# A last matrix product with the two halves of its moving operand side by side, and the sums of a block at other slots

## The chip, the core and the metric

The kernel runs on one core of a Trainium2 chip. The metric is the device time of one execution in microseconds. Three runs of the kernel before took 1485.69, 1486.63 and 1486.93 us; the median is 1486.63 us.

## What is computed

A retention layer (attention with a decay in place of a softmax), then two feed-forward layers over 4608 tokens. The change touches only the last product, `g @ w_out` of the second one.

```
x = attention output, (4608, 512)                     # 8 batches of 576 positions, 8 heads of 64
h = (x @ w1) * (x @ w2) @ w3;  x2 = h @ w_out         # 512 -> 1024 -> 512
h = x2 @ w_in                                         # 512 -> 2048
g = h * clip(h + 3, 0, 6) / 6
out = g @ w_out2                                      # 2048 -> 512
```

All inputs are normal random numbers times a scale.

## The kernel before

Precision. TensorE multiplies in a format with a shorter mantissa than float32 (float32r). Each operand is therefore split into a high and a low part, `hi` (ScalarE casts the value) and `lo` (VectorE subtracts `hi` from the value), and a product is the sum of three matmuls: hi x hi, hi x lo and lo x hi. The helper `mm3` (lines 123 to 127) issues these three, each with its own load of the stationary operand.

The last product. The 2x2 block products of `g @ w_out2` are formed with seven products in place of eight (a Strassen form). `out_block(b)` (lines 886 to 930) makes 256 tokens, and there are 18 blocks. In a block, product p (0 to 6) has an operand made from four pieces of g (128 tokens by 1024 features each, called `raw`, one load each) and their sums as the stationary side, and a prepared matrix T of w_out2 as the moving side, 1024 x 256 as `hi` and `lo`. Line 920 cuts from T, for each of the eight steps kt of 128 features, 512 columns: 256 of `hi` and 256 of `lo` beside them. Line 921 gives the two halves to `mm3` as two moving operands of 256 columns. A step is thus three loads and three matmuls of 256 columns; a block has 7 x 8 = 56 steps and the stage 18 x 56 = 1008.

Banks. Four PSUM banks A, B, C and D take the seven products: A products 0 and 3, B product 1, D products 2 and 5, C products 4 and 6. Where a bank is used twice, the second product adds to what is there, after the first result has been read. Before, 256 of the 512 columns of a bank are used. The pool has eight banks, so a block and the next one use different ones. After each product its bank is read: by ScalarE (a copy) for products 0 and 3 (lines 923 and 925), by VectorE (an add of the bank to an earlier result, line 695) for the other five. The results are `u`, `U = u + B`, `V = U + D` and four pieces of the output; after products 5 and 6 SP's queue stores 128 tokens each (line 900).

Operands. `prep(b, p, s)` (lines 835 to 854) makes `hi` (line 845, ScalarE) and `lo` (line 849, VectorE, through line 130) of product p, 128 x 1024 values each; it is called two products ahead. There are three pairs of operand tiles, so the tile of product p + 2 is that of product p - 1. `s_sum(b, i)` (lines 825 to 831) is one of four sums of a block, 128 x 1024 values on VectorE: sums 1 and 2 go to the units 1 and 2 for products 2 and 1, sum 3 to unit 1 for product 4, sum 4 to unit 1 for product 5. `load_raw` (line 813) loads a piece of the next block on SP's queue.

Order. The kernel is scheduled by hand. Every step begins with a tick; `at(s, f)` (line 113) says that f is issued at tick s, ahead of the matmuls of that step, and engines run their instructions in the order of issue. The read of a product stands at the tick after its last step; `hi` one tick and `lo` three ticks after the start of the product in which they are prepared; sums 3 and 4 at the start of products 2 and 3 (line 852), sums 1 and 2 of the next block five ticks into products 4 and 5 (line 916); the loads of the next block at the start of product 0 (three pieces) and four ticks into product 3 (one).

Of the kernel before, what the change touches and what calls it, by code (L numbers as in the profile page):

```python
# [7 lines left out]
F32 = mybir.dt.float32  # L8
# [18 lines left out]
def retention_moe_kernel(  # L27
# [20 lines left out]
    nc = tc.nc  # L48
# [61 lines left out]
    now = [0]  # L110
    ready = set()

    def at(s, f):
        slots.setdefault(max(s, now[0]), []).append(f)

    def tick():
        q_ = slots.get(now[0], [])
        while q_:
            q_.pop(0)()
        slots.pop(now[0], None)  # L120
        now[0] += 1

    def mm3(out_ap, sh, sl, mh, ml, first, last, **kw):
        tick()
        nc.tensor.matmul(out=out_ap, lhsT=sh, rhs=mh, start=first, stop=False, **kw)  # L125
        nc.tensor.matmul(out=out_ap, lhsT=sh, rhs=ml, start=False, stop=False, **kw)  # L126
        nc.tensor.matmul(out=out_ap, lhsT=sl, rhs=mh, start=False, stop=last, **kw)  # L127

    def sub(eng, out_ap, x, y):
        eng.tensor_tensor(out=out_ap, in0=x, in1=y, op=ALU.subtract)  # L130
# [45 lines left out]
    A, Bh = slice(0, 64), slice(64, 128)  # L176
# [125 lines left out]
    with tc.manual_schedule():  # L302
# [155 lines left out]
        for n, (i, j) in enumerate(w3_order()):  # L458
            if j == 0:
                Wps[i] = ps_mm.tile([128, DM], F32, tag="mm", name="Wps")  # L460
            ps = Wps[i]
# [3 lines left out]
                             start=j == 0, stop=j == KF - 1)  # L465
# [219 lines left out]
        ps = ctx.enter_context(tc.tile_pool(name="ps", bufs=8, space=PSUM))  # L685
# [8 lines left out]
        def add(out_ap, a, b):  # L694
            nc.vector.tensor_tensor(out=out_ap, in0=a, in1=b, op=ALU.add)  # L695
# [106 lines left out]
        def f32_unit(k):  # L802
            if k not in un:
                un[k] = ring(k, [128, 1024], F32, "unit")
            return un[k]

        def raw(b, h, kh):
            return f32_unit(RAW[(4 * b + PARTS.index((h, kh))) % 7])

        def load_raw(b, h, kh):  # L810
            if b < NB3:
                p0 = 256 * b + 128 * h
                nc.sync.dma_start(out=raw(b, h, kh).rearrange("p (m t) -> p m t", t=128), in_=gd[:, 8 * kh:8 * kh + 8, p0:p0 + 128])

        def op_tiles(q):
            i = q % 3
            if i not in ops:
                if i == 0:
                    ops[i] = [wf_p.tile([128, 1024], F32R, tag="wr", name="op") for _ in range(2)]
                else:  # L820
                    x = xo_p.tile([128, 2, 1024], F32R, tag=("xh", "xl")[i - 1], name="op")
                    ops[i] = [x[:, 0], x[:, 1]]
            return ops[i]

        def s_sum(b, i):
            if b < NB3:
                o, x, y, f = (
                    (1, (1, 0), (1, 1), ALU.add), (2, 1, (0, 0), ALU.subtract),
                    (1, (0, 0), (1, 0), ALU.subtract), (1, (0, 1), 2, ALU.subtract))[i - 1]
                t = [f32_unit(v) if isinstance(v, int) else raw(b, *v) for v in (x, y)]  # L830
                nc.vector.tensor_tensor(out=f32_unit(o), in0=t[0], in1=t[1], op=f)  # L831
# [3 lines left out]
        def prep(b, p, s):  # L835
            b, p = b + p // 7, p % 7
            if b == NB3:
                return
            c = {}

            def src():
                return f32_unit(SRC[p]) if isinstance(SRC[p], int) else raw(b, *SRC[p])

            def hi():
                nc.scalar.copy(out=op_tiles(7 * b + p)[0], in_=src())  # L845

            def lo():
                h, l = op_tiles(7 * b + p)
                sub(nc.vector, l, src(), h)

            if p in (4, 5):
                at(s, lambda: s_sum(b, p - 1))
            at(s + 1, hi)
            at(s + 3, lo)

        for sb in range(NSB):
            for k, n in enumerate(SETS):
                if (sb, k) == (NSB - 1, 7):
                    s = now[0]
                    at(s + 5, lambda: s_sum(0, 2))  # L860
                    prep(0, 1, s + 9)
                    at(s + 9, lambda: load_raw(0, 0, 1))
                run_set(sb, n)
                if sb < NSB - 1:
                    k0 = 3 if sb == 0 else 2
                    if k0 <= k < k0 + 4:
                        load_xop(sb + 1, k - k0)
                    if k == 7:
                        for i in range(4, 7):
                            at(now[0], lambda i=i, sb=sb: load_xop(sb + 1, i))  # L870
                else:
                    if 1 <= k <= 4:
                        q_tile(k - 1)
                    if k == 2:
                        for part in PARTS[:3]:
                            load_raw(0, *part)
                    if k == 4:
                        s_sum(0, 1)
                    if k == 5:
                        prep(0, 0, now[0])  # L880
                    if k > 4:
                        q_late(k - 5)
# [3 lines left out]
        def out_block(b):  # L886
            c = {}
            z = b % 2
            o = [stg[:, 1024 * z + 512 * h:1024 * z + 512 * h + 512] for h in range(2)]
            u, U, V = (stg_hi[:, 512 * i + 256 * z:512 * i + 256 * z + 256] for i in range(3))  # L890
            p0 = 256 * b

            def bank(k):
                c[k] = ps.tile([128, 512], F32, tag="b", name="po")[:, 0:256]

            def store(h):
                hh, g = divmod((p0 + 128 * h) % (2 * BLK), BLK)
                g += (p0 + 128 * h) // (2 * BLK) * BLK
                r0 = g // HB1 * BLK1 + hh * HB1 + g % HB1
                nc.sync.dma_start(out=out[r0:r0 + 128, :], in_=o[h])  # L900

            def add2(out_ap, a, k):
                return lambda: add(out_ap, a, c[k])

            for p, (k, first) in enumerate((
                    ("A", True), ("B", True), ("D", True), ("A", False), ("C", True), ("D", False), ("C", False))):
                if first:
                    bank(k)
                if p == 0:
                    for part in PARTS[:3]:  # L910
                        at(now[0], lambda part=part: load_raw(b + 1, *part))
                if p == 3:
                    at(now[0] + 4, lambda: load_raw(b + 1, 0, 1))
                prep(b, p + 2, now[0])
                if p in (4, 5):
                    at(now[0] + 5, lambda p=p: s_sum(b + 1, p - 3))
                h, l = op_tiles(7 * b + p)
                for kt in range(8):
                    ts = slice(128 * kt, 128 * kt + 128)
                    w = tq[p, kt // 2][:, 512 * (kt % 2):512 * (kt % 2) + 512]  # L920
                    mm3(c[k], h[:, ts], l[:, ts], w[:, 0:256], w[:, 256:512], first and kt == 0, kt == 7, skip_group_check=True)
                if p == 0:
                    at(now[0], lambda: nc.scalar.copy(out=u, in_=c["A"]))
                elif p == 3:
                    at(now[0], lambda: nc.scalar.copy(out=o[0][:, 256:512], in_=c["A"]))
                else:
                    at(now[0], add2(*{1: (U, u, "B"), 2: (V, U, "D"), 4: (o[1][:, 0:256], V, "C"),
                                      5: (o[0][:, 0:256], U, "D"), 6: (o[1][:, 256:512], U, "C")}[p]))
                if p > 4:
                    at(now[0] + 1, lambda p=p: store(p - 5))  # L930

        for b in range(NB3):
            out_block(b)
# [66 lines left out]
```

## Time and profile before

| | |
|---|---|
| runs | 1485.69, 1486.63, 1486.93 us |
| the profiled execution's own time | 1486.61 us |
| its span, first to last instruction | 1484.7 us |
| mean granted TensorE clock | 0.999 of full speed |
| TensorE matmul / weight load busy | 1469.7 / 1313.3 us |
| VectorE / ScalarE / GpSimd busy | 956.4 / 568.8 / 254.2 us |
| matmuls of the last product | first at 1118.19 us, last at 1480.95 us |

PE stands for TensorE's matmuls, PEld for its weight loads, DVE for VectorE, ACT for ScalarE, POOL for GpSimd, SP for SyncE. A letter q behind a name is that engine's queue of DMA issues. Matmuls are pipelined: the duration of one is longer than the distance to the next, so that distances have to be read from the starts. L695 is line 695 of the kernel; a line can be that of a helper, and then the names of the tiles tell the use: `po` is a bank of the last product, `op` an operand tile, `unit` a piece of g or a sum, `wq` the matrix T, `stg` and `stghi` hold results. The kernel and the numbers of its lines are those of before.

### The profile page before, as it was taken

The numbers are of one execution on the slowest core, as the hardware profiler recorded it, in microseconds if no ns is written. First come the engines' busy times: TensorE is split into PE (matmuls) and PEld (weight loads), VectorE is DVE, ScalarE is ACT, GpSimd is POOL, SyncE is SP. The second block draws the span as 40 slices with busy tenths as digits, with TensorE's granted clock in tenths as the row PEclk, the third lists the DMA queues.
The fourth block names the chain that finished last, engine by engine and source line by source line (L and its number), as shares of the span: only waits on it lengthen the run. The fifth ranks groups of instructions, "written<-read, shape, count | busy, mean of one in ns | idle before, by whom it ended". The sixth has DMA issues, their size and how long they took to land. (4 is left out here: it accounts for less than half of the span.)

```text
span 1484.7 us, 26113 instructions
## 1 busy us (share of the span) xinstructions
PE 1469.7 (99%) x10544; PEld 1313.3 (88%) x10544; DVE 956.4 (64%) x1617; ACT 568.8 (38%) x857; POOL 254.2 (17%) x461
## 2 busy tenths in 40 slices
PE   9999999999999999999999999999999999999999
PEld 5478888888888888888889999999999999999998
DVE  6886566566564746574545666666667777777775
ACT  6563333233333333332433333333334333333332
POOL 3313212222222111110012322232220000000000
PEclk9999999999999999999999999999999999999999
DMA  9963657565565556554799753644698444455441
GB/s 327 264 179 107 204 166 190 180 178 191 170 191 155 198 163 194 168 163 140 261 354 348 280 221 149 256 175 189 241 389 253 131 127 120 122 142 143 138 131 45
DMA packets 186586, 287.34 MB, mean 194 GB/s; under 512 B 12528, under 2 KB 143600, under 8 KB 184928
## 3 DMA queue, kind: packets, MB, share of 16 engines
q1 hardware_dynamic: 103584, 151.01, 31.1%
q0 software_dynamic: 25856, 75.93, 16.6%
q10 hardware_dynamic: 57024, 58.73, 11.9%
q8 instruction: 83, 1.36, 0.4%
q14 instruction: 39, 0.32, 0.1%
HBM read 176.04 MB, written 109.58 MB: 192 GB/s over the span
## 5 line engine op out<-in xcount | busy, mean ns | idle before, releaser
L125 PE MATMUL po<-wq,op 128*128 128x256 f32 x1008 | 285.3, 283 | 0.0
L126 PE MATMUL po<-wq,op 128*128 128x256 f32 x1008 | 285.3, 283 | 0.0
L127 PE MATMUL po<-wq,op 128*128 128x256 f32 x1008 | 285.3, 283 | 0.0
L125 PE MATMUL pb<-xop,wset 128*128 128x384 f32 x672 | 226.2, 337 | 5.6 <-DVE stghi L695 2.4
L127 PE MATMUL pb<-xop,wset 128*128 128x384 f32 x672 | 225.8, 336 | 0.0
L126 PE MATMUL pb<-xop,wset 128*128 128x384 f32 x672 | 225.6, 336 | 0.0
L130 DVE TENSOR_TENSOR op<-unit,op 128x1024 fp32r<-128x1024 f32 x126 | 154.1, 1224 | 92.8 <-ACT op L845 92.8
L845 ACT CAST op<-unit 128x1024 fp32r<-128x1024 f32 x126 | 132.2, 1049 | 186.1 <-DVE unit L831 164.6
L127 PEld LDWEIGHTS po<-wq,op 128*128 128x128 f32 x1008 | 193.5, 192 | 0.0
L126 PEld LDWEIGHTS po<-wq,op 128*128 128x128 f32 x1008 | 193.5, 192 | 0.0
L125 PEld LDWEIGHTS po<-wq,op 128*128 128x128 f32 x1008 | 193.5, 192 | 0.0
L714 POOL DMA_DIRECT2D gd<-g x192 | 103.9, 541 | 348.7 <-DVE g L709 223.4
L186 POOL DMA_DIRECT2D qk<-in_qk_dram x144 | 84.3, 592 | 434.2 <-PE z L233 360.8
L705 ACT ACTIVATE stghi<-g,half 128x384 f32<-128x384 f32 x141 | 87.1, 617 | 132.7 <-DVE g L695 132.7
L125 PEld LDWEIGHTS pb<-xop,wset 128*128 128x128 f32 x672 | 126.2, 188 | 8.3 <-DVE stghi L695 3.0
L126 PEld LDWEIGHTS pb<-xop,wset 128*128 128x128 f32 x672 | 126.2, 188 | 0.0
L127 PEld LDWEIGHTS pb<-xop,wset 128*128 128x128 f32 x672 | 126.2, 188 | 0.0
L125 PE MATMUL pa<-xh,w1h 128*128 128x512 f32 x288 | 114.1, 396 | 0.0
L125 PE MATMUL px<-abh,Wh 128*128 128x512 f32 x288 | 114.0, 396 | 0.0
L126 PE MATMUL pa<-xl,w1h 128*128 128x512 f32 x288 | 112.2, 390 | 0.6 <-DVE xl L130 0.6
L125 PE MATMUL pb<-xh,w2h 128*128 128x512 f32 x288 | 112.3, 390 | 0.0
L127 PE MATMUL pa<-xh,w1l 128*128 128x512 f32 x288 | 112.2, 390 | 0.0
(137 smaller groups left out, 2542.1 us busy)
## 6 DMA issues: line engine op xcount, KB each, us to landing
gd<-g POOLq DMA_DIRECT2D x192, 192.0 KB, 4.0
unit<-gd SPq DMA_DIRECT2D x72, 512.0 KB, 5.7
xop<-xod SPq DMA_DIRECT2D x42, 768.0 KB, 9.0
qk<-in_qk_dram POOLq DMA_DIRECT2D x144, 128.0 KB, 4.6
wset<-wid SPq DMA_DIRECT2D x8, 1792.0 KB, 12.7
wr<-in_w_dram SPq DMA_DIRECT2D x24, 512.0 KB, 12.9
kv<-in_kv_dram POOLq DMA_DIRECT2D x36, 256.0 KB, 5.1
kv<-in_kv_dram POOLq DMA_DIRECT2D x72, 128.0 KB, 4.9
```

Source lines behind the costliest of these rows:

```text
L125: nc.tensor.matmul(out=out_ap, lhsT=sh, rhs=mh, start=first, stop=False, **kw)
L126: nc.tensor.matmul(out=out_ap, lhsT=sh, rhs=ml, start=False, stop=False, **kw)
L127: nc.tensor.matmul(out=out_ap, lhsT=sl, rhs=mh, start=False, stop=last, **kw)
L130: eng.tensor_tensor(out=out_ap, in0=x, in1=y, op=ALU.subtract)
L186: nc.gpsimd.dma_start(out=x[rows, g].rearrange("d x a i -> d x (a i)"), in_=qk[2 * t + g].rearrange("d x (b a) i -> d x b (a i)", a=2)[:, ...
L705: nc.scalar.activation(out=c["r"], in_=src(), func=ACTF.Relu, bias=half, scale=1.0 / 6.0)
L714: nc.gpsimd.dma_start(out=gd[:, m, p0:p0 + BLK], in_=c["g"])
L845: nc.scalar.copy(out=op_tiles(7 * b + p)[0], in_=src())
```

## The change

- A step of the last product is two matmuls in place of three: `hi` of the operand against 512 columns of T (its `hi` and `lo` side by side), written to all 512 columns of the bank, and `lo` of the operand against the 256 columns of T's `hi`, added to the first half of the bank.
- A result is then the sum of both halves of a bank. VectorE adds the first half (or ScalarE copies it, for products 0 and 3), and a second add on VectorE puts the other half on top, in place.
- Sum 3 of a block is issued five ticks into product 1 and sum 4 five ticks into product 2, in place of the start of products 2 and 3. Sums 1 and 2 of the next block keep their places.

```diff
@@ prep
-            if p in (4, 5):
-                at(s, lambda: s_sum(b, p - 1))
             at(s + 1, hi)
             at(s + 3, lo)
@@ out_block
-                c[k] = ps.tile([128, 512], F32, tag="b", name="po")[:, 0:256]
+                c[k] = ps.tile([128, 512], F32, tag="b", name="po")
...
             def add2(out_ap, a, k):
-                return lambda: add(out_ap, a, c[k])
+                def f():
+                    y = c[k][:, 256:512]
+                    if a is None:
+                        nc.scalar.copy(out=out_ap, in_=c[k][:, 0:256])
+                    else:
+                        add(out_ap, a, c[k][:, 0:256])
+                    add(out_ap, out_ap, y)
+                return f
...
-                if p in (4, 5):
-                    at(now[0] + 5, lambda p=p: s_sum(b + 1, p - 3))
+                if p in (1, 2, 4, 5):
+                    at(now[0] + 5, lambda p=p: s_sum(b + p // 4, p % 3 + 2 - p // 4 * 2))
...
-                    mm3(c[k], h[:, ts], l[:, ts], w[:, 0:256], w[:, 256:512], first and kt == 0, kt == 7, skip_group_check=True)
-                if p == 0:
-                    at(now[0], lambda: nc.scalar.copy(out=u, in_=c["A"]))
-                elif p == 3:
-                    at(now[0], lambda: nc.scalar.copy(out=o[0][:, 256:512], in_=c["A"]))
-                else:
-                    at(now[0], add2(*{1: (U, u, "B"), 2: (V, U, "D"), 4: (o[1][:, 0:256], V, "C"),
-                                      5: (o[0][:, 0:256], U, "D"), 6: (o[1][:, 256:512], U, "C")}[p]))
+                    tick()
+                    nc.tensor.matmul(out=c[k], lhsT=h[:, ts], rhs=w, start=first and kt == 0, stop=False, skip_group_check=True)
+                    nc.tensor.matmul(out=c[k][:, 0:256], lhsT=l[:, ts], rhs=w[:, 0:256], start=False, stop=kt == 7, skip_group_check=True)
+                at(now[0], add2(*{0: (u, None, "A"), 1: (U, u, "B"), 2: (V, U, "D"), 3: (o[0][:, 256:512], None, "A"),
+                                  4: (o[1][:, 0:256], V, "C"), 5: (o[0][:, 0:256], U, "D"), 6: (o[1][:, 256:512], U, "C")}[p]))
```

## Rows read from the trace of the kernel before

**Rows 1.** The page: busy time by engine, and the granted clock in 40 slices.
```profile
PE 1469.7 (99%) x10544; PEld 1313.3 (88%) x10544; DVE 956.4 (64%) x1617; ACT 568.8 (38%) x857; POOL 254.2 (17%) x461
...
PEclk9999999999999999999999999999999999999999
```

**Rows 2.** Windows: busy time by engine in the last stage and inside it.
```profile
core 0: us, PE busy (x) PEld busy (x) DVE busy (x) ACT busy (x) POOL busy (x), PEclk, DMA share, GB/s
1118.36:1480.60 362.24, 362.24 (x3021) 362.24 (x3021) 261.23 (x287) 138.81 (x162) 1.65 (x4) 1.00 0.46 134
...
1200.00:1220.00 20.00, 20.00 (x169) 20.00 (x168) 14.53 (x17) 7.62 (x10) 0.00 (x0) 1.00 0.44 129
```

**Rows 3.** Timeline of TensorE, last stage: start, duration, engine, line, operation.
```profile
1118.19 0.28 PE L125 MATMUL po<-wq,op 128*128 128x256 f32 x1
1118.31 0.28 PE L126 MATMUL po<-wq,op 128*128 128x256 f32 x1
1118.43 0.28 PE L127 MATMUL po<-wq,op 128*128 128x256 f32 x1
1118.55 0.28 PE L125 MATMUL po<-wq,op 128*128 128x256 f32 x1
...
1480.95 0.28 PE L127 MATMUL po<-wq,op 128*128 128x256 f32 x1
```

**Rows 4.** Groups by line: count, busy us, mean ns, idle before and its releaser.
```profile
L125 PE MATMUL po<-wq,op 128*128 128x256 f32 x1008 | 285.3, 283 | 0.0
...
L125 PEld LDWEIGHTS po<-wq,op 128*128 128x128 f32 x1008 | 193.5, 192 | 0.0
L130 DVE TENSOR_TENSOR op<-unit,op 128x1024 fp32r<-128x1024 f32 x126 | 154.1, 1224 | 92.8 <-ACT op L845 92.8
L845 ACT CAST op<-unit 128x1024 fp32r<-128x1024 f32 x126 | 132.2, 1049 | 186.1 <-DVE unit L831 164.6 <-ACT op L845 11.9 <-PE po L126 5.7
...
L695 DVE TENSOR_TENSOR stg<-stghi,po 128x256 f32<-128x256 f32 x54 | 22.4, 415 | 4.6 <-PE po L127 4.6
...
L695 DVE TENSOR_TENSOR stghi<-stghi,po 128x256 f32<-128x256 f32 x36 | 15.0, 417 | 5.4 <-PE po L127 5.4
```

**Rows 5.** Timeline of TensorE, earlier stages: 18 intervals at 384 columns, 24 at 512.
```profile
899.81 0.33 PE L125 MATMUL pb<-xop,wset 128*128 128x384 f32 x1
...
902.92 0.34 PE L125 MATMUL pb<-xop,wset 128*128 128x384 f32 x1
...
700.11 0.39 PE L125 MATMUL pa<-xh,w1h 128*128 128x512 f32 x1
...
705.55 0.39 PE L125 MATMUL pa<-xh,w1h 128*128 128x512 f32 x1
```

**Rows 6.** Timeline of VectorE, fifth block of the last stage.
```profile
1204.79 0.42 DVE L695 TENSOR_TENSOR stghi<-stghi,po 128x256 f32<-128x256 f32 x1 [0.30 <-PE po L127]
1205.13 1.22 DVE L831 TENSOR_TENSOR unit<-unit 128x1024 f32<-128x1024 f32 x1
...
1213.78 1.22 DVE L831 TENSOR_TENSOR unit<-unit 128x1024 f32<-128x1024 f32 x1
1214.92 0.41 DVE L695 TENSOR_TENSOR stg<-stghi,po 128x256 f32<-128x256 f32 x1
1215.25 1.22 DVE L130 TENSOR_TENSOR op<-unit,op 128x1024 fp32r<-128x1024 f32 x1
1216.38 1.22 DVE L831 TENSOR_TENSOR unit<-unit 128x1024 f32<-128x1024 f32 x1
```

**Rows 7.** Timeline of VectorE, sums of an earlier stage.
```profile
712.96 0.42 DVE L610 TENSOR_TENSOR stg<-stg 128x256 f32<-128x256 f32 x1
...
713.42 1.09 DVE L610 TENSOR_TENSOR stg<-stg 128x256 f32<-128x256 f32 x3
```

**Rows 8.** Timeline of ScalarE in the fifth block, and DMA issues (KB, us to landing).
```profile
1201.91 0.37 ACT L923 COPY stghi<-po 128x256 f32<-128x256 f32 x1 [1.90 <-PE po L127]
1202.18 1.05 ACT L845 CAST op<-unit 128x1024 fp32r<-128x1024 f32 x1
1206.45 1.05 ACT L845 CAST op<-unit 128x1024 fp32r<-128x1024 f32 x1 [3.23 <-DVE unit L831]
...
unit<-gd SPq DMA_DIRECT2D x72, 512.0 KB, 5.7
```

**Rows 9.** Waits of SP's queue in the last stage: us in total, times, longest.
```profile
SPq L813 <- DVE unit L831: 57.8, 16, 4.1
```

**Rows 10.** Timeline, end of the kernel.
```profile
1481.27 0.42 DVE L695 TENSOR_TENSOR stg<-stghi,po 128x256 f32<-128x256 f32 x1 [2.45 <-PE po L127]
1481.71 0.33 SPq L900 DMA_DIRECT2D out_dram<-stg  x1
```

## The prediction

> **What bounds the kernel now.** I read the page first. TensorE is busy for 99% of the span, VectorE for 64%, and the granted clock is full (the 2.4 GHz level) in all 40 slices [rows 1]. So only work that leaves TensorE can shorten the kernel, and VectorE has room on average only. The change touches the last stage, so I asked for the windows of that stage: in 362.24 us TensorE has 362.24 us of busy time, at clock 1.00; in a stretch of 20 us inside it VectorE is busy for 14.53 us and ScalarE for 7.62 us [rows 2]. A busy TensorE need not be at its peak, so the next view is the timeline of its matmuls: their starts, not their durations. The stage's matmuls of 256 columns start every 0.12 us from the first at 1118.19 to the last at 1480.95 [rows 3]. That is 3 x 1008 = 3024 matmuls [rows 4] and 3023 intervals, 362.76 / 3023 = 120.0 ns each, without a gap. TensorE never waits for anything here; the stage is exactly its own issue period times its count.
>
> What is in 120 ns? 256 columns at 2.4 GHz are 106.7 ns. Earlier stages issue the same triple at other widths. At 384 columns, 18 intervals take 3.11 us, 172.8 ns each, against 160.0 for the columns; at 512 columns, 24 intervals take 5.44 us, 226.7 ns each, against 213.3 [rows 5]. The rest is 13.3, 12.8 and 13.3 ns: a fixed price of one matmul with its weight load, the same at every width. Each matmul has a load of its own in these rows (1008 for each of the three lines, busy 192 ns and overlapped) [rows 4].
>
> **TensorE's part.** The change replaces three pairs of load and matmul per step (256 + 256 + 256 columns) by two (512 + 256). The columns stay 768; one load and one fixed price go. By the periods just read a step takes 226.7 + 120.0 = 346.7 ns in place of 360.0. There are 1008 steps: 1008 x 13.3 = **13.4 us less**. The rows show each width only in a run of its own kind, so the mixed run has to be bounded. Above: 360 ns, nothing comes back. Below: 333.3 ns, if the narrow matmul's load hid wholly behind the wide one before it, so that both prices went (26.9 us less). I take 346.7, because at 512 columns each load already has a wide matmul in front of it and the 13.3 ns are still there, and at 256 the load also fits at that price.
>
> The Trainium skill, page "TensorE: Matmul & The Clock Gate", section "Back-to-back issue gap", gives the gap of a lone matmul as its columns at 2.4 GHz plus about 2.5 ns. By that a step would lose only 2.5 ns, 2.5 us in all. The trace differs: 13.3 ns for a matmul with its load, at both widths [rows 3, 5]. What is left of that rule is the third rival.
>
> **VectorE's part.** Seven results per block of 256 tokens now need two halves of a bank. Five of them (U, V and three output pieces) get a second add of 128x256; the two that ScalarE copies out get a first one. That is 7 per block, 126 in 18 blocks. An add of this shape with one operand in PSUM lasts 415 to 417 ns [rows 4], but between instructions that don't depend on each other VectorE starts the next one early: from 0.41 us adds to what follows it is 0.33 us, and from a 1.22 us subtraction to what follows 1.14 us (1213.78 to 1214.92, 1215.25, 1216.38) [rows 6]. The second add of a pair reads what the first wrote. The nearest rows for that are the sums of 256 columns in an earlier stage, where the second needs the first's result: 712.96 to 713.42, 0.46 us [rows 7]. So a new add costs 0.33 to 0.46 us. For a block: 5 x 0.46 + 2 x 0.33 = 2.96 us. Before, VectorE is busy for 14.53 / 20 x 20.16 = 14.65 us of a block (168 matmuls of 120 ns); after, 17.6 us of 56 x 0.3467 = 19.41 us, a share of 91%. It fits, with 1.8 us to spare, and the 126 x 0.42 = 53 us of new busy time cost nothing as long as TensorE doesn't meet its queue.
>
> Where it can meet it: (a) the operands of product p+2 are prepared during product p, so each has about one product (2.77 us) of slack; (b) a bank that is read after one product and accumulated into by a later one. A (products 0 and 3) and D (2 and 5) have two products between, C (4 and 6) only one. There the second half's add must have read C before product 6 starts. Step VectorE's queue from a block's start, products starting every 2.77 us, with ScalarE's copies of 1.05 us and the distances between instructions of [rows 6, 8]. ScalarE copies A's first half at 2.97 (0.2 us behind the product's end, as U's add now) and starts product 3's operand at 3.24; its subtraction runs from 4.33 to 5.47; the third sum to 6.61; U's adds until 7.4; the copy for product 4, which waits for the third sum, runs from 6.79 to 7.84, its subtraction from 7.88 to 9.02; the fourth sum to 10.16; V's adds to 10.95; the copy for product 5 starts 0.1 us after the sum's end and ends at 11.39, its subtraction ends at 12.57; the half of A at 12.9; product 6's subtraction at 14.05; the next block's first sum at 15.19; then C's two adds, done at 16.06. Product 6 starts at 6 x 2.77 = 16.64. **Margin 0.58 us.** In the trace of before the fifth block starts at 1118.19 + 4 x 20.16 = 1198.83 and its product 6 at 1198.83 + 6 x 2.88 = 1216.11; C's add starts at 1214.92 and lasts 0.41 [rows 6], a margin of 0.78 us, and TensorE didn't wait. So the doubled adds use up little of it, because the sums moved.
>
> **The moved sums.** The third and fourth sum of a block go from the head of products 2 and 3 to five steps into products 1 and 2. Eleven long instructions per block stay eleven; only their order changes. Now ScalarE waits 164.6 us for sums [rows 4], which is idle time of an engine off the path. They are put ahead of U's and V's adds, so the adds wait for up to 1.1 us and the operand copies don't. Without the move the operand of product 5 would stand behind U's and V's double adds. The unit that the third sum frees is refilled by a load on SP's queue (that queue waits 57.8 us for sums [rows 9]); it comes earlier, so nothing there gets worse. Stores wait for an add up to half a us longer; behind them on SP stand loads of the next block, which land in 5.7 us [rows 8] and are needed more than 10 us later. ScalarE gets no new instruction; its copy of A at products 0 and 3 now has VectorE's add behind it, 0.4 us, and the subtraction queued there waits for ScalarE's next copy anyway.
>
> **The end.** The last result gets its second add after the last matmul, with nothing to cover it: 0.46 us before the store at 1481.71 [rows 10].
>
> **Sum.** The profiled execution took 1486.61 us (span 1484.70, 1.9 around it), within 0.02 us of the median of 1486.63. 1486.6 - 13.4 + 0.5 = **1473.6 us**, 0.9% less. A measurement of this kernel can tell about 0.2% (3 us) from no change.
>
> **Rivals.**
> 1. *Bank C is read late, a little.* If each of the seven new adds of a block cost 0.3 us more than reckoned (a semaphore between the two adds beyond the 0.46), that is 2.1 us against 1.8 to spare, and TensorE waits 0.3 us per block in front of product 6: 18 x 0.3 = 5.4 us, so **1479 us**. For it: 91% load and only one product's time. Against: the row of dependent adds [rows 7]. Chance 0.10.
> 2. *VectorE becomes the bound* (the other side). Same place, further on: a new add that costs 0.5 us more makes 3.5 us against 1.8, 1.7 us of waiting per block, 18 x 1.7 = 30.6 us: 1473.6 + 30.6 = **1504 us**. It decides once the wait eats the 0.75 us that a block gains, (1.8 + 0.75) / 7 = 0.36 us more, so from about 0.8 us for a new add. For it: VectorE already stands idle for 92.8 us in front of operand subtractions, waiting for ScalarE's copies [rows 4], so the 1.8 us may not all be usable. Against: that idle time is in what I stepped through. Chance 0.08.
> 3. *The fixed price stays*: the 13.3 ns belong to something other than the pair, say to each 256 columns written in this stage. Then a step keeps 360 ns and only the end's 0.5 us come: **1487.1 us**, no change. The Trainium skill's gap on the page named above would give 1484.6. Against: three widths on one line. Chance 0.04.
> 4. *Both prices go*: 1486.6 - 26.9 + 0.5 = **1460.2 us**. Chance 0.03.
>
> **How the numbers follow.** The forecast as reckoned, within a us (run to run 1485.69 to 1486.93), has the remaining 0.75. The range reaches from 1472.5 (a us below the forecast) to 1480.0, which takes in the first rival to its middle and a little beyond; left out are the second, third and fourth and the rest of the first, 0.19 in all. Faster by over 0.2%: 0.75 + 0.09 of the first + 0.03 of the fourth, with 0.01 of the third (where a part of the price goes), 0.88. Within 0.2%: 0.03 of the third, and 0.02 of the first and second where the wait just cancels the gain, 0.05. Slower: 0.07, the rest of the second.
>
> **What would show it.** In the timeline after, each step of the last stage starts 0.347 us after the one before; the stage takes 349.4 us; 2016 matmuls and as many loads in it. VectorE's busy time in a 20 us stretch rises from 14.5 to about 18 us. No wait of TensorE for an add of bank C: if its idle time in front of product 6 is seen 18 times, the first or second rival is right, and its length says which. A step of 360 ns without idle time is the third; 333 ns the fourth. If the wait lies in front of an operand's subtraction instead, my stepping of the moved sums was wrong.

## The result and the profile after

The kernel after took 1473.21, 1473.64, 1473.84 and 1474.79 us, median 1473.74 us, against 1486.78 us for the kernel before in the same comparison: a ratio of 0.9908 with a 95% interval of 0.9896 to 0.9919. The forecast was 1473.6 us, range 1472.5 to 1480.0. The profiled execution took 1473.84 us with a span of 1472.1 us.

The page of the kernel after, busy time by engine, VectorE's 40 slices, and two of its groups (count; busy us, mean ns; idle before):

```profile
PE 1456.9 (99%) x9536; PEld 1259.6 (86%) x9536; DVE 1006.2 (68%) x1743; ACT 567.8 (39%) x857; POOL 254.2 (17%) x461
...
DVE  6886566656464747464545666666668998889897
...
L927 PE MATMUL po<-wq,op 128*128 128x512 f32 x1008 | 349.5, 391 | 0.0
L928 PE MATMUL po<-wq,op 128*128 128x256 f32 x1008 | 282.2, 280 | 0.0
...
L130 DVE TENSOR_TENSOR op<-unit,op 128x1024 fp32r<-128x1024 f32 x126 | 154.1, 1223 | 32.7 <-ACT op L845 32.7
```

Against [rows 1] there are 1008 matmuls and loads fewer and 126 VectorE instructions more, and VectorE's share is eight or nine tenths in the last ten slices, but for the very last. VectorE's idle time in front of the operand subtractions falls from 92.8 us [rows 4] to 32.7: the new adds fill it. (The move of the sums alone leaves it at 95.4, in the run with only the sums moved.) The two kinds of matmul have no idle time before them.

The timeline of TensorE in the last stage, first steps and last step (L927 is the wide matmul, L928 the narrow one):

```profile
1118.51 0.39 PE L927 MATMUL po<-wq,op 128*128 128x512 f32 x1
1118.74 0.28 PE L928 MATMUL po<-wq,op 128*128 128x256 f32 x1
1118.86 0.39 PE L927 MATMUL po<-wq,op 128*128 128x512 f32 x1
...
1467.60 0.39 PE L927 MATMUL po<-wq,op 128*128 128x512 f32 x1
1467.83 0.28 PE L928 MATMUL po<-wq,op 128*128 128x256 f32 x1
1468.15 0.42 DVE L695 TENSOR_TENSOR stg<-stghi,po 128x256 f32<-128x256 f32 x1 [1.89 <-PE po L928]
1468.60 0.42 DVE L695 TENSOR_TENSOR stg<-stg,po 128x256 f32<-128x256 f32 x1
```

1007 intervals from 1118.51 to 1467.60 are 346.66 ns each, for 360.0 before [rows 3]. From the first matmul to the last the stage takes 349.32 us in place of 362.76, 13.44 us less. The last add now starts 0.77 us behind the last matmul and not 0.32: the second add costs 0.45 us in the open. The stage began 0.32 us later in this execution than in that of before. -13.44 + 0.45 + 0.32 = -12.67 us, and the spans differ by 12.6 us.

Where VectorE's new work went, in the windows of the kernel after (the columns are those of [rows 2]):

```profile
1200.00:1220.00 20.00, 20.00 (x118) 17.62 (x117) 17.55 (x24) 8.20 (x10) 0.00 (x0) 1.00 0.51 139
1300.00:1320.00 20.00, 20.00 (x117) 17.62 (x117) 18.00 (x25) 8.29 (x10) 0.00 (x0) 1.00 0.50 142
```

14.53 us of 20 became 17.55 to 18.00, and TensorE is busy for the whole of both windows. VectorE's timeline in the fifth block, from the third sum to the adds that free bank C:

```profile
1201.63 1.22 DVE L831 TENSOR_TENSOR unit<-unit 128x1024 f32<-128x1024 f32 x1
1202.77 0.87 DVE L695 TENSOR_TENSOR stghi<-stghi,po 128x256 f32<-128x256 f32 x2
1204.05 1.23 DVE L130 TENSOR_TENSOR op<-unit,op 128x1024 fp32r<-128x1024 f32 x1 [0.41 <-ACT op L845]
1205.31 1.23 DVE L831 TENSOR_TENSOR unit<-unit 128x1024 f32<-128x1024 f32 x1
...
1210.33 1.22 DVE L831 TENSOR_TENSOR unit<-unit 128x1024 f32<-128x1024 f32 x1
1211.47 0.41 DVE L695 TENSOR_TENSOR stg<-stghi,po 128x256 f32<-128x256 f32 x1
1211.92 0.42 DVE L695 TENSOR_TENSOR stg<-stg,po 128x256 f32<-128x256 f32 x1
```

The block starts at 1118.51 + 4 x 56 x 0.34667 = 1196.16. The third sum starts 5.47 us into it (forecast 5.47), and C's second add ends at 1212.34, 16.18 us into it (forecast 16.06). Product 6 starts at 16.64, so the margin is 0.46 us (forecast 0.58). The 0.12 us between them lie at one place: the fourth sum starts 1.26 us behind the subtraction ahead of it (1204.05 to 1205.31), not 1.14, and all that follows is late by that. Dependent adds stand 0.45 us apart (forecast 0.46).

### The profile page after: what moved, and what is told of

Its sections match the earlier page's. It is cut to its first block, busy times and chain, and to the rows that moved or that the text cites. A ratio compares the mean times of both kernels' runs of the same rounds, so it can differ in the third digit from the quotient of the medians.

```text
span 1472.1 us, 24291 instructions
## 1 busy us (share of the span) xinstructions
PE 1456.9 (99%) x9536; PEld 1259.6 (86%) x9536; DVE 1006.2 (68%) x1743; ACT 567.8 (39%) x857; POOL 254.2 (17%) x461
## 5 line engine op out<-in xcount | busy, mean ns | idle before, releaser
L927 PE MATMUL po<-wq,op 128*128 128x512 f32 x1008 | 349.5, 391 | 0.0
L928 PE MATMUL po<-wq,op 128*128 128x256 f32 x1008 | 282.2, 280 | 0.0
L927 PEld LDWEIGHTS po<-wq,op 128*128 128x128 f32 x1008 | 188.5, 187 | 41.3
L928 PEld LDWEIGHTS po<-wq,op 128*128 128x128 f32 x1008 | 190.5, 189 | 0.0
L130 DVE TENSOR_TENSOR op<-unit,op 128x1024 fp32r<-128x1024 f32 x126 | 154.1, 1223 | 32.7 <-ACT op L845 32.7
L127 PE MATMUL px<-abh,Wl 128*128 128x512 f32 x288 | 112.2, 390 | 0.0
L126 PE MATMUL px<-abl,Wh 128*128 128x512 f32 x288 | 112.1, 389 | 0.0
```

The lines of the kernel that those rows point to most:

```text
L927: nc.tensor.matmul(out=c[k], lhsT=h[:, ts], rhs=w, start=first and kt == 0, stop=False, skip_group_check=True)
L928: nc.tensor.matmul(out=c[k][:, 0:256], lhsT=l[:, ts], rhs=w[:, 0:256], start=False, stop=kt == 7, skip_group_check=True)
```

## The experiments

The experiments ran in later comparisons. In those the median of the kernel before was 1487.08 to 1487.83 us, and the kernel after was not run again. A ratio is to the kernel before in the same comparison; a difference from the 1473.74 us of the kernel after is good to about a microsecond.

**The sums back at their old places.** The kernel after, with this edit:

```diff
+            if p in (4, 5):
+                at(s, lambda: s_sum(b, p - 1))
             at(s + 1, hi)
...
-                if p in (1, 2, 4, 5):
-                    at(now[0] + 5, lambda p=p: s_sum(b + p // 4, p % 3 + 2 - p // 4 * 2))
+                if p in (4, 5):
+                    at(now[0] + 5, lambda p=p: s_sum(b + 1, p - 3))
```

> The merged matmuls and both adds as in the kernel after; the third and fourth sum of a block back at the head of products 2 and 3. Theory (VectorE's adds are hidden only because the sums were moved): U's and V's double adds now stand ahead of the sums, the operands of products 5 and 6 and the read of bank C come late, and TensorE waits at products 5 and 6 of each block, by stepping the queues with the rows' distances 1.3 us per block, 23 us in all: about 1497 us, slower than before. Rival (VectorE's 17.6 us of work per 19.4 us fit in any order): 1473.7 us.

It took 1502.97 us, ratio 1.0101 (1.0086 to 1.0116). The waits in the last stage of that kernel, for TensorE's loads and for its matmuls (L929 wide, L930 narrow; us in total, times, longest):

```profile
PEld po L929 <- issue: 15.9, 17, 1.0
PEld po L930 <- DVE op L130: 9.6, 18, 0.6
...
PE po L929 <- DVE stg L695: 10.4, 16, 0.7
PE po L930 <- DVE op L130: 3.6, 16, 0.3
```

Two places, once per block each: the `lo` operand of product 5, and the read of bank C in front of product 6. These are the two that had been named. Without the move the change would be 1% slower than the kernel before: the second half of the edit carries the first. VectorE has the same work in both kernels and is less busy here (16.50 us in the window from 1200 to 1220), so the order decides and not the sum. From its first wide matmul to its last, TensorE takes 27.6 us more than in the kernel after: by the distances of the starts, 23.8 of them lie in the steps with a wait, and 3.8 in the steps between, which take 350.6 ns on average in place of 346.7. These come up again further down.

**Only the sums moved.** The kernel before with the sums at their new places, three matmuls and single adds.

> The kernel before with only the third and fourth sum moved; three matmuls of 256 columns and single adds as before. Theory: TensorE had no wait to lose, so 1486.6 us, within 0.2 percent of before. Rival (a part of the 13 us comes from the new order): 1480 us or less.

1488.09 us against 1487.7, ratio 1.0002 (0.9992 to 1.0011). The move alone is worth nothing that could be measured: TensorE had no wait to lose.

**Three pairs in the new layout.** The kernel after, with the wide matmul cut in two:

```diff
-nc.tensor.matmul(out=c[k], lhsT=h[:, ts], rhs=w, start=first and kt == 0, stop=False, skip_group_check=True)
+nc.tensor.matmul(out=c[k][:, 0:256], lhsT=h[:, ts], rhs=w[:, 0:256], start=first and kt == 0, stop=False, skip_group_check=True)
+nc.tensor.matmul(out=c[k][:, 256:512], lhsT=h[:, ts], rhs=w[:, 256:512], start=False, stop=False, skip_group_check=True)
```

> The kernel after with the wide matmul cut into two of 256 columns, each with its own load, into the two halves of the bank; both adds and the moved sums stay. Theory (a fixed price of 13.3 ns per pair of load and matmul): a step takes 360 ns again, the last product 362.9 us, in all 1486.6 + 0.5 = 1487.1 us. Rival (the gain comes from the bank's layout or from two halves written in turn, not from the pair): near 1473.7 us.

1488.05 us, ratio 1.0002 (0.9992 to 1.0011). Its timeline, three matmuls of one step and the start of the next:

```profile
1199.72 0.28 PE L927 MATMUL po<-wq,op 128*128 128x256 f32 x1
1199.84 0.28 PE L928 MATMUL po<-wq,op 128*128 128x256 f32 x1
1199.96 0.28 PE L929 MATMUL po<-wq,op 128*128 128x256 f32 x1
1200.08 0.28 PE L927 MATMUL po<-wq,op 128*128 128x256 f32 x1
```

The same columns, banks, adds and sums, with one pair of load and matmul more, are back at 360 ns. The whole gain is that pair. Whether the 13.3 ns belong to its load or to its matmul isn't shown: every matmul here has a load of its own, and no run separates the two.

**A third pair that is narrow.** The kernel after, with the narrow matmul cut into two of 128 columns.

> The kernel after with the matmul of the low part (256 columns) cut into two of 128 columns, each with its load: columns as before, three pairs per step. Theory (a fixed 13.3 ns per pair at any width): 360 ns per step, 1487 us. Rival (a pair can't be shorter than its load takes, and 256 columns happen to hide one, so that a pair of 128 columns still takes about 120 ns): 226.7 + 2 x 120 = 466.7 ns per step, 1008 x 120 = 121 us more than after, about 1595 us.

1584.64 us, ratio 1.0653 (1.0632 to 1.0674). The timeline of TensorE and its loads there, one step and the start of the next:

```profile
1200.27 0.19 PEld L927 LDWEIGHTS po<-wq,op 128*128 128x128 f32 x1
1200.32 0.45 PE L927 MATMUL po<-wq,op 128*128 128x512 f32 x1
1200.38 0.43 PEld L929 LDWEIGHTS po<-wq,op 128*128 128x128 f32 x2
1200.61 0.33 PE L929 MATMUL po<-wq,op 128*128 128x128 f32 x2
1200.72 0.19 PEld L927 LDWEIGHTS po<-wq,op 128*128 128x128 f32 x1
1200.78 0.45 PE L927 MATMUL po<-wq,op 128*128 128x512 f32 x1
```

A step is 456.6 ns on average, 110 ns more than after and not 13.3. So the fixed price is not the whole law: with the wide matmul at its 226.7 ns, 115 ns are left on average for each narrow pair, where its 128 columns and 13.3 ns would be 66.7. The rival's 120 is near the size. But the rows show no even split: the first narrow matmul starts 0.29 us behind the wide one (1200.32 to 1200.61; 0.23 in the kernel after), and the next wide one 0.17 us behind that, for both narrow ones. That the load is what can't hide behind 128 columns is argued and not shown; no run varies it. The 13.3 ns hold at 256, 384 and 512 columns, which is all that the forecast needed.

**Extra adds ahead of bank C's read, and behind it.** In the kernel after the first add of one product's result is issued four times (the output stays the same):

```diff
-                        add(out_ap, a, c[k][:, 0:256])
+                        for _ in range(1 + more):
+                            add(out_ap, a, c[k][:, 0:256])
```

with `more` = 3 at product 4 (ahead), or 3 at product 5 (behind), or 1 at all five.

> The kernel after with the first add of product 4's result (the read of bank C) issued four times in place of once, 3 x 0.33 = 1.0 us more of VectorE per block, ahead of the read that frees bank C. Theory (what counts is that C's adds end before product 6, with a margin of 0.45 us in the trace of after): product 6 waits 0.45 us in nearly every block, by stepping the queues 8 us in all, about 1482 us. Rival (only VectorE's sum per block counts, 18.6 of 19.4 us): 1473.7 us.

> The kernel after with the same three extra adds at product 5's result, so behind the read that frees bank C and not ahead of it. Theory (the place in the queue decides): the delay is worked off before the next read of C and TensorE never waits, 1473.7 us. Rival (the sum per block decides, and three adds more cost what they cost ahead of C): about 1482 us.

> The kernel after with the first add of each of the five results that VectorE reads issued twice: five adds more per block, 5 x 0.33 = 1.7 us, about all that VectorE has to spare, but only one of them between product 4 and the read of C. Theory (place, not sum): TensorE hardly waits, by stepping the queues 0 us, 1473.7 to 1476 us. Rival (the sum decides): 1.7 us more per block are more than e4's 1.0 us, so over 1482 us.

Ahead: 1495.44 us, ratio 1.0047 (1.0032 to 1.0061). Behind: 1481.7 us, 0.9956 (0.9942 to 0.997). One more each: 1481.2 us, 0.996 (0.9945 to 0.9975). The same three adds cost some 22 us in one place and 8 in the other, so place matters as the theory has it; but all three runs came out 5 us or more above it, and the runs with the adds behind C and with one more each came out near the times of their rivals, if not by their cause. The traces tell how. With the adds ahead of C, VectorE and TensorE in the fifth block (L928 wide, L929 narrow):

```profile
1217.17 1.78 DVE L695 TENSOR_TENSOR stg<-stghi,po 128x256 f32<-128x256 f32 x4
1218.98 0.42 DVE L695 TENSOR_TENSOR stg<-stg,po 128x256 f32<-128x256 f32 x1
...
1218.39 0.28 PE L929 MATMUL po<-wq,op 128*128 128x256 f32 x1
1219.55 0.47 PE L928 MATMUL po<-wq,op 128*128 128x512 f32 x1 [0.88 <-DVE stg L695]
```

Four adds take 1.78 us, 0.45 us apart and not 0.33: each overwrites the output of the one before, and costs what a dependent add costs. Three more are 1.36 us, 0.9 us over the margin of 0.46, and TensorE waits 0.88 us here. That is twice what had been reckoned, and explains some 16 us of the 22; the steps between the waits are longer too (351.5 ns on average, 4.7 us in all). Behind C, TensorE should not wait, and in a later stretch it doesn't. Windows of that kernel, and of the one with an add more each:

```profile
1320.00:1340.00 20.00, 20.00 (x116) 17.35 (x115) 18.75 (x28) 7.83 (x9) 0.00 (x0) 1.00 0.47 134
```

```profile
1320.00:1340.00 20.00, 20.00 (x116) 17.33 (x115) 19.54 (x30) 7.94 (x10) 0.00 (x0) 1.00 0.48 136
```

TensorE is busy throughout at full clock, yet issues 116 matmuls where the kernel after issues 117 or 118. By the groups of the bank's tile, the wide matmuls of the run with the adds behind C start from 1119.6 to 1475.4: 355.8 / 1007 = 353.3 ns per step, 6.7 ns more. The waits in it are few and early: half a us in the second block, for the `lo` operand of product 1 (so the theory's "never waits" failed there), then 0.11 and 0.07 us at bank C. Its first block has 346.9 ns per step, and all blocks from the fourth on have 353.3 without a wait.

With an add more each, the one that lies ahead of C costs 0.45 us, which is the margin of 0.46. Product 6 comes 0.07, 0.16 and 0.14 us late in the first three blocks and not again. The wide matmuls at the second and the third of these waits:

```profile
1154.79 0.39 PE L928 MATMUL po<-wq,op 128*128 128x512 f32 x1
1155.30 0.47 PE L928 MATMUL po<-wq,op 128*128 128x512 f32 x1
1155.72 0.39 PE L928 MATMUL po<-wq,op 128*128 128x512 f32 x1
...
1156.76 0.39 PE L928 MATMUL po<-wq,op 128*128 128x512 f32 x1
...
1174.44 0.39 PE L928 MATMUL po<-wq,op 128*128 128x512 f32 x1
1174.92 0.47 PE L928 MATMUL po<-wq,op 128*128 128x512 f32 x1
1175.34 0.39 PE L928 MATMUL po<-wq,op 128*128 128x512 f32 x1
...
1176.40 0.40 PE L928 MATMUL po<-wq,op 128*128 128x512 f32 x1
```

Behind the second wait three steps take 1.04 us (1155.72 to 1156.76, 347 ns each), as before it; behind the third 1.06 (1175.34 to 1176.40, 353 ns), and so to the end of the stage. All four runs with waits so far had longer steps somewhere behind them. So the next theory was that a wait leaves something behind.

**One wait.** The three extra adds at product 4 of a single block, the first or the tenth.

> The kernel after with three extra adds ahead of the read of bank C in the first block only, so that TensorE waits once, about 1.2 us, in front of product 6 of block 0. Theory (in the runs with waits the steps behind a wait were some 6.7 ns longer, 353.4 in place of 346.7 ns, and stayed so until the next wait): with nothing to set it right, 17 blocks of 56 steps at 6.7 ns, 6.4 us beside the wait, so about 1481 us. Rival (the longer steps come from VectorE's extra work while it lasts): only the wait, 1475 us.

> The same single wait in the tenth block. Theory: steps of 346.7 ns before it and of about 353.4 ns after it, 8 blocks x 56 x 6.7 ns = 3.0 us beside the wait of 1 us, about 1478 us. Rival: only the wait, 1475 us.

In the first block: 1481.73 us, ratio 0.9962 (0.9947 to 0.9976). In the tenth: 1476.59 us, 0.9924 (0.9908 to 0.9941). Windows of the run with the wait in the tenth block, one before it and two behind it, and its timeline at the wait (L928 wide, L929 narrow):

```profile
1200.00:1220.00 20.00, 20.00 (x117) 17.62 (x116) 17.63 (x24) 8.12 (x10) 0.00 (x0) 1.00 0.48 139
1320.00:1340.00 20.00, 20.00 (x115) 17.38 (x114) 17.68 (x24) 7.82 (x9) 0.00 (x0) 1.00 0.50 143
1400.00:1420.00 20.00, 20.00 (x115) 17.32 (x115) 17.68 (x24) 8.05 (x10) 0.00 (x0) 1.00 0.48 137
```

```profile
1308.06 0.39 PE L928 MATMUL po<-wq,op 128*128 128x512 f32 x1
...
1309.10 0.39 PE L928 MATMUL po<-wq,op 128*128 128x512 f32 x1
...
1310.84 0.47 PE L928 MATMUL po<-wq,op 128*128 128x512 f32 x1 [0.89 <-DVE stg L695]
...
1311.61 0.40 PE L928 MATMUL po<-wq,op 128*128 128x512 f32 x1
...
1312.67 0.40 PE L928 MATMUL po<-wq,op 128*128 128x512 f32 x1
```

Before the wait three steps take 1.04 us (347 ns each), behind it 1.06 (353 ns), and it stays so to the end, with VectorE's extra work long over. That refutes the rival for these two profiled runs: the wait costs its own length and then 6.7 ns on every step that follows. A wait is not certain to do so: the four times with the wait in the tenth block are 1475.01, 1475.25, 1477.93 and 1478.54 us, two near the rival's 1475 and two near the theory's 1478. The early wait gave 1480.71 to 1483.07 in all four. The trace of the run with the sums back shows the same inside one execution: behind its 17 waits at bank C the steps are 353 ns after eleven and 346.7 after six, longer and shorter mixed. So a wait seems to decide anew how the steps behind it go, and a later wait can end the longer ones.

**One wait in the form with three pairs, and with the narrow matmul first.** The same single wait (six extra adds) in the form of three matmuls of 256 columns; and the single early wait with the two matmuls of a step exchanged.

> The form with three matmuls of 256 columns (the wide one cut in two) with six extra adds ahead of the read of C in the first block only, so that TensorE waits once for a us or two. Theory (longer steps after a wait belong to the mixture of a wide and a narrow matmul): steps of 360 ns before and after, 1488 us plus the wait. Rival (any stream of matmuls falls into longer steps after a wait): steps of about 367 ns after it, 6 us more.

> The single early wait as in the run with one wait in block 0, with the narrow matmul issued ahead of the wide one in every step. Theory (the longer steps come with any mixture of a wide and a narrow matmul): about 353 ns per step after the wait, 1481 us. Rival (they come from this order, in which a bank's new product begins with the wide matmul and its wait): 346.7 ns per step after the wait, 1475 us.

Three pairs: 1489.69 us, ratio 1.0012 (1.0002 to 1.0022). Its windows behind the wait, which lies near 1138:

```profile
1200.00:1220.00 20.00, 20.00 (x169) 20.00 (x168) 17.29 (x24) 7.89 (x9) 0.00 (x0) 1.00 0.45 132
1400.00:1420.00 20.00, 20.00 (x169) 20.00 (x168) 17.30 (x24) 7.89 (x9) 0.00 (x0) 1.00 0.47 133
```

169 matmuls as in [rows 2]: 120.0 ns behind a wait of 1.6 us as ahead of it. All eight times (1488.37 to 1490.46) lie around the theory's 1488 us and the wait, 5 us or more below what longer steps would give. The longer steps don't belong to any wait in any stream; of the two streams tried, only the mixed one has them. Narrow first: median 1476.1 us, ratio 0.9941 (0.9918 to 0.9963), from 1474.49, 1475.65, 1476.54 and 1481.84 us. Its profiled run had steps of 346.7 ns behind the wait, but the time of 1481.84 is what the longer steps give. Four times don't settle whether the order helps.

**The end.** The kernel after with bank C of the last block alone in the old form (three matmuls, one half, a single add).

> The kernel after with bank C of the last block alone (products 4 and 6) in the old form: three matmuls of 256 columns into one half and a single add. Theory: 16 steps pay 13.3 ns more (0.21 us), the second add behind the last matmul is gone (0.45 us), so the span is 0.24 us shorter than that of after, too little for the times to show. Rival (the add at the end is hidden behind something): the span is 0.2 us longer.

The median of two times is 1475.05 us, ratio 0.9916 (0.9897 to 0.9936), and the span 1472.1 us, as after: neither shows 0.24 us, and the form is no gain that can be measured. The expected span didn't come, since this stage began 0.25 us later, at 1118.76. From there to the last store's issue are 350.35 us (1469.11 - 1118.76), against 350.54 in the kernel after (1469.05 - 1118.51): 0.19 us less, close to the theory. No version that ran is measurably faster than the kernel after.

## Why the prediction was right

*The fixed price per pair* was read from distances between starts at three widths [rows 3, 5] and carried the forecast: 346.7 ns foretold, 346.66 measured, and 360 ns again as soon as a third pair returned. The busy times could not have told it: the two groups of matmuls are busy for 349.5 + 282.2 us, overlapped, in a stage of 349.3 us. The mixed run showed neither bound: not 360, not 333.3.

*The second add's price* of 0.46 us, from rows of another stage [rows 7], is 0.45 in the last stage; VectorE's window of about 18 us came at 17.55 to 18.00.

*The stepping of VectorE's queue* to bank C gave a margin of 0.58 us; it is 0.46. It rightly named bank C as the place that decides, and the reason for the moved sums: with them back, TensorE waits at products 5 and 6 and the kernel is some 29 us slower than after. Run by run this is the most useful part of the prediction, since an average load of 90% fits both a kernel that gains 13 us and one that loses 15.

*The end* cost 0.45 us (0.46 foretold).

That the time agrees to 0.1 us is in part luck: the start of this stage, ahead of which nothing was changed, lies anywhere from 1117.38 to 1119.60 us in the traces.

*The rivals.* The small wait at C and VectorE as the bound did not happen, but their price was put too low: the prediction counted only the length of the wait. One wait of about a us early in the stage costs 8 us in all (1481.7 against 1473.7), because the steps behind it lengthen. Waits far shorter than the first rival's 0.3 us did as much: three of 0.07 to 0.16 us were followed by 1481.2 us. So the first rival would have cost up to 6 us beside its 5.4. The fixed price did not stay, and not both went.

The Trainium skill, page "TensorE: Matmul & The Clock Gate", section "Back-to-back issue gap", gives about 2.5 ns beside the columns for a lone matmul. For a matmul with a load of its own the trace shows another price, 13.3 ns at 256 and at 512 columns.

Still open: what in TensorE keeps the longer steps going, why one wait brings them on and another doesn't, whether the 13.3 ns belong to the load or to the matmul, and what the 110 ns of the step with two matmuls of 128 columns are.

## What to carry to other kernels

Where each matmul has its own load, read the price of the pair from the distance of starts at two widths; joining two products with the same stationary operand saves that price once per step, as long as the output fits a bank. Pay for it on another engine only after stepping that engine's queue to the read that frees the next bank: the order of the same work decided some 29 us here. And keep a dense mixed stream free of even one wait, be it of 0.14 us; it may cost more behind it than it lasts.

## What had not been expected of the hardware

A stream of wide and narrow matmuls (512 and 256 columns, each with a load) ran at 346.7 ns per step as long as it never waited. Behind a wait, of a us or of only 0.14, it often ran at 353.3 ns until the next wait or the end of the stage, with the granted clock at 1.00 and no idle time in the profile; behind other waits of the same execution it went on at 346.7. The step in which the wait ended stood 0.42 us long as well (1310.84 to 1311.27). A stream of 256 columns alone went back to 120.0 ns behind its one wait.
